# How the rows of two heads of W_o are split over the transfer engines, and x is loaded in four pieces

## The chip, the cores and the metric

The kernel runs on one core of a Trainium2 chip. The core has five compute queues that the profile names PE (TensorE, matrix multiplication), PEld (its weight loads), DVE (VectorE), ACT (ScalarE) and POOL (GpSimd), and SP, whose queue in this kernel does nothing but issue transfers. Transfers between the chip's memory (HBM) and the core's on-chip memory are carried by 16 transfer engines, which the profile calls the core's 16 DMA engines. Each works through its own share of the issued transfers.

The metric is device time in microseconds (us) of one execution. The time given for a kernel is the median over several executions.

## The reference, cut to what matters

One decoding step of a transformer block for two sequences (B = 2, one token each, D = 512): attention over a cache of 8192 positions with 32 heads of 128, and then a gated feed-forward layer of width 1376. Everything is bfloat16.

```python
def _A_ref(x, k_cache, v_cache, wq, wo):          # k_cache, v_cache: 2 x 32 x 8192 x 128
    q = (x @ wq).reshape(B, 1, 32, 128).transpose(0, 2, 1, 3)
    scores = einsum("bhqd,bhkd->bhqk", q, k_cache) * 128 ** -0.5
    o = einsum("bhqk,bhkd->bhqd", softmax(scores), v_cache)
    return o.transpose(0, 2, 1, 3).reshape(B, 1, 4096) @ wo
...
def _B_ref(x, W_gate, W_up, W_down):
    gate, up = x @ W_gate, x @ W_up
    return (gate * (gate > 0) * up) @ W_down
...
h  = x + _A_ref(layernorm(x), k_cache, v_cache, wq, wo)
h2 = h + _B_ref(layernorm(h), W_gate, W_up, W_down)
```

The caches are 2 x 128 MiB and each byte is read once. W_o is 4096 x 512: rows 128*h to 128*h + 127 belong to head h.

## The kernel before, in words

**Stages.** The caches come as 15 tiles of four heads each (8 MiB of K and 8 MiB of V a tile, 64 KB for each of the 128 partitions), and the last four heads of the second sequence as two half tiles, called p0 and p1 in the code. Three buffers of 64 KB per partition hold them in turn. For each tile DVE multiplies K by the query (`products`, L375), adds along the head dimension by halving (`scores`, L393 and L395), TensorE does a part of the positions itself (`scores_pe`), ACT takes exponentials, and TensorE multiplies with V (`values`, L446). When the caches are through, the weights W_o, W_gate, W_up and W_down are loaded into parts of the buffers that have come free, the attention's output is multiplied with W_o (`attend_set`, L502, and `attend`, L509), and the feed-forward layer follows: W_gate (`g_ps`, L686), W_up (`u_ps`, L686) and W_down (`d_ps`, L719).

**Order.** The order of every instruction on every queue is written out by hand in the source (`tc.manual_schedule()`). A transfer is issued when SP reaches it in its queue and the buffer that it writes is free; from there its packets stand in the transfer engines' own queues behind those issued earlier. There are eight semaphores for the completion of transfers, which the 56 transfers of the program use in turn; a transfer that finds its semaphore not yet at rest waits on SP for the earlier one.

**x.** x (2 x 512) is loaded as five rows onto two partitions, issued from ACT's queue (L190): per sequence pieces of 256 elements, the last piece of the second sequence cut into two of 128. TensorE transposes it (L238), the layer norm and the projection with W_q follow, and the first product with K waits for the projected query (`qrep`).

**W_o.** The rows are loaded in sets of heads (`SETS`: 16, 8, 4 and 2 heads, then heads 30 and 31 alone). In a set of n heads partition p holds n successive rows of W_o, so that each partition reads one contiguous piece of n KB; `load_set` (L567) issues it as 128 rows. The attention's output has to be laid out in the same way: `spread` (L481, one DVE instruction for each set and sequence) writes a head's column times a pattern of zeros and ones (`quot`), and `lay_rows` (L492, L496) multiplies that with the pattern `rest` on TensorE and copies the result to `orow`. Heads 30 and 31 are loaded plainly, row r of the head on partition r, and need no such layout. Head 31's load (L590) is written with its rows in four groups of 32, `[[P // 4 * D, 4], [D, P // 4], [1, D]]`; the groups follow each other without a gap in memory.

**W_down.** Its last chunk is loaded in three pieces of 32 partitions (L616), the other ten chunks in sets of 5, 3, 1 and 1 (L621).

Of the kernel before, what the change touches and what calls it, by code (L numbers as in the profile page):

```python
# [8 lines left out]
ALU = mybir.AluOpType  # L9
# [4 lines left out]
def _free(t, offset, dims):  # L14

    return bass.AP(tensor=t.tensor, offset=t.offset + offset, ap=[t.ap[0]] + [list(d) for d in dims])


def _dram(t, offset, dims):
    return bass.AP(tensor=t.tensor, offset=t.offset + offset, ap=[list(d) for d in dims])  # L20
# [3 lines left out]
def kernel(  # L24
# [13 lines left out]
    nc = tc.nc  # L38
    P = nc.NUM_PARTITIONS
    B, Sq, D = A_x.shape  # L40
    _, Hkv, Sk, Dh = A_k_cache.shape
    Hq = A_wq.shape[1] // Dh
# [24 lines left out]

    SETS = [(0, 16, 0), (16, 8, 16), (24, 4, 24), (28, 2, 28)]
    HM = 30
    SROWS = [n for _, n, _ in SETS]  # L70


# [15 lines left out]
    ocol = front.tile([P, Hq, B], bf16)  # L88
# [5 lines left out]
    qrep = consts.tile([P, LASTQ + 2, Dh], bf16)  # L94
# [17 lines left out]
    hm = consts.tile([P, FC, B], bf16)  # L112
    quot = {r: consts.tile([P, Dh // r], bf16, name=f"quot{r}") for r in SROWS}
    rest = {r: consts.tile([P, r], bf16, name=f"rest{r}") for r in SROWS}
    orow = [consts.tile([P, r, B], bf16, name=f"orow{k}") for k, r in enumerate(SROWS)]
    sel = consts.tile([B, B, P // 2], bf16)
# [8 lines left out]
    wo = bufs[0][:, HALF:TILE]  # L125
# [34 lines left out]
    def load_tile(cache, s, dst, pieces=1):  # L160
        h = NH * s.g + (0 if s.quad else 2 * s.k)
        n = s.nt * Dh
        w = n // pieces
        for k in range(pieces):
            nc.sync.dma_start(
                out=dst[:, k * w:(k + 1) * w], in_=_dram(cache, (s.b * Hkv + h) * Sk * Dh + k * w, [[n, P], [1, w]]),
            )

    def ln_cols(src, dst_bkc, pfx):

        m_ps = ps.tile([P, B, KC], f32, tag="mx")
        nc.tensor.matmul(out=m_ps, lhsT=mean_w, rhs=src, start=True, stop=True)
        mean = small.tile([P, B], f32, tag=pfx + "mean")
        nc.vector.tensor_reduce(out=mean, in_=m_ps, axis=AXIS.X, op=ALU.add)
        dev = small.tile([P, B, KC], f32, tag=pfx + "dev")
        nc.vector.tensor_tensor(out=dev, in0=src, in1=_free(mean, 0, [[1, B], [0, KC]]), op=ALU.subtract)
        sq = small.tile([P, B, KC], f32, tag=pfx + "sq")
        nc.vector.tensor_tensor(out=sq, in0=dev, in1=dev, op=ALU.mult)
        v_ps = ps.tile([P, B, KC], f32, tag="mx")
        nc.tensor.matmul(out=v_ps, lhsT=mean_w, rhs=sq, start=True, stop=True)  # L180
        rstd = small.tile([P, B], f32, tag=pfx + "rstd")
        nc.vector.tensor_reduce(out=rstd, in_=v_ps, axis=AXIS.X, op=ALU.add)
        nc.scalar.activation(out=rstd, in_=rstd, func=ACT.Sqrt, bias=eps_col, scale=1.0)
        nc.vector.reciprocal(out=rstd, in_=rstd)
        nc.vector.tensor_tensor(out=dst_bkc, in0=dev, in1=_free(rstd, 0, [[1, B], [0, KC]]), op=ALU.mult)

    with tc.manual_schedule():

        for b, k, n in ((0, 0, 2), (0, 2, 2), (1, 0, 2), (1, 2, 1), (1, 3, 1)):
            nc.scalar.dma_start(  # L190
                out=xr[b:b + 1, k * P:(k + n) * P], in_=_dram(A_x, b * D + k * P, [[D, 1], [1, n * P]]),
            )
# [9 lines left out]
            out=nscale, in_=nscale, compare_op=ALU.not_equal, fill=-SCALE,  # L202
# [5 lines left out]
            out=ident_f, in_=ident_f, compare_op=ALU.not_equal, fill=1.0,  # L208
# [4 lines left out]
            out=sel, in_=sel, compare_op=ALU.not_equal, fill=1.0,  # L213
# [9 lines left out]
            out=pick, in_=pick, compare_op=ALU.not_equal, fill=1.0,  # L223
# [17 lines left out]
        ln_cols(xc, xn.rearrange("p c b -> p b c"), "l1")  # L241
        for r in SROWS:
            nc.vector.tensor_reduce(out=rest[r], in_=_free(ident, 0, [[1, r], [r, P // r]]), axis=AXIS.X, op=ALU.max)
# [4 lines left out]
        for g0 in range(0, NQ, 4):  # L248
            for n0 in range(NH * g0 * Dh, NH * (g0 + 4) * Dh, 4 * Dh):
                q_ps = ps2.tile([B, 4 * Dh], f32, tag="o")  # L250
                for c in range(KC):
                    nc.tensor.matmul(  # L252
                        out=q_ps, lhsT=xn[:, c, :], rhs=wq_sb[:, c, n0:n0 + 4 * Dh], start=(c == 0), stop=(c == KC - 1),
                    )
                nc.vector.tensor_copy(qrow[:, n0:n0 + 4 * Dh], q_ps)
            for b in range(B):
                r_ps = ps2.tile([P, 4, Dh], f32, tag="tp")
                for j in range(NH):
                    nc.tensor.matmul(
                        out=r_ps[j * (P // NH):(j + 1) * (P // NH)], lhsT=sel[:, b, 0:P // NH],  # L260
# [5 lines left out]
        for j in range(2):  # L266
            nc.tensor.matmul(
                out=r_ps[j * (P // 2):(j + 1) * (P // 2)], lhsT=sel[:, B - 1, :],
# [116 lines left out]
        def scores(s):  # L385

            scol = scols[s.i]
            width = Dh
            while width > 8:
                half = width // 2  # L390
                lo = _free(s.kt, s.na * Dh, [[Dh, s.nv - s.na], [1, half]])
                hi = _free(s.kt, s.na * Dh + half, [[Dh, s.nv - s.na], [1, half]])
                nc.vector.tensor_tensor(out=lo, in0=lo, in1=hi, op=ALU.add)  # L393
                width = half
            nc.vector.tensor_reduce(  # L395
                out=scol[:, s.na:s.nv], in_=_free(s.kt, s.na * Dh, [[Dh, s.nv - s.na], [1, 8]]), axis=AXIS.X, op=ALU.add,
            )
            pms[s.i] = small.tile([P, 1], f32, tag="pm", name="pm", bufs=2)
            nc.vector.tensor_reduce(out=pms[s.i], in_=scol, axis=AXIS.X, op=ALU.max)  # L399
# [76 lines left out]
        def spread(k, b):  # L476

            h0, n, _ = SETS[k]
            nq = Dh // n
            sp = qrep[:, B * k + b, :]  # L480
            nc.vector.tensor_tensor(  # L481
                out=_free(sp, 0, [[nq, n], [1, nq]]), in0=_free(ocol, h0 * B + b, [[B, n], [0, nq]]),
                in1=_free(quot[n], 0, [[0, n], [1, nq]]), op=ALU.mult,
            )
            return sp

        def lay_rows(k, sps, scalar=False):

            r = SROWS[k]
            or_ps = ps.tile([P, B, r], f32, tag="mx")  # L490
            for b in range(B):
                nc.tensor.matmul(out=or_ps[:, b, :], lhsT=sps[b], rhs=rest[r], start=True, stop=True)  # L492
            if scalar:
                nc.scalar.activation(out=orow[k], in_=or_ps.rearrange("p b c -> p c b"), func=ACT.Copy)
            else:
                nc.vector.tensor_copy(orow[k], or_ps.rearrange("p b c -> p c b"))  # L496

        def attend_set(k, r0=0, r1=None):
            for c0 in range(r0, SROWS[k] if r1 is None else r1):
                for c in range(KC):  # L500
                    at = (SETS[k][2] + c0) * D + c
                    nc.tensor.matmul(  # L502
                        out=att_ps[:, c, :], lhsT=_free(wo, at, [[KC, P]]), rhs=orow[k][:, c0, :],
                        start=(k == 0 and c0 == 0 and c == 0), stop=False, skip_group_check=True,
                    )
# [9 lines left out]
        for i in range(Q):  # L515
# [21 lines left out]
            half = s.nt // VG // 2  # L537
# [27 lines left out]
        def load_set(k):  # L565
            h0, n, at = SETS[k]
            nc.sync.dma_start(  # L567
                out=wo[:, at * D:(at + n) * D], in_=_dram(A_wo, h0 * Dh * D, [[n * D, P], [1, n * D]]),
            )
# [14 lines left out]

        scores_pe(p0, values_and_sums)
        load_tile(A_v_cache, p1, p1.vt)
        for k in range(1, len(SETS)):
            load_set(k)
        nc.sync.dma_start(out=wo[:, HM * D:(HM + 1) * D], in_=_dram(A_wo, HM * Dh * D, [[D, P], [1, D]]))
        nc.sync.dma_start(  # L590
            out=wo[:, (HM + 1) * D:Hq * D], in_=_dram(A_wo, (HM + 1) * Dh * D, [[P // 4 * D, 4], [D, P // 4], [1, D]]),
        )
        scores(p0)

        def first():
# [15 lines left out]
        for w, src in ((0, B_W_gate), (1, B_W_up)):  # L611
            nc.sync.dma_start(
                out=wgu[:, w].rearrange("p c f -> p (c f)"), in_=_dram(src, 0, [[KC * F, P], [1, KC * F]]),
            )
        for q0 in range(AGAIN, P, AGAIN):
            nc.sync.dma_start(  # L616
                out=wd_sb[q0:q0 + AGAIN, FC - 1, :], in_=_dram(B_W_down, (F - P + q0) * D, [[D, AGAIN], [1, D]]),
            )
        for f0, n in FSETS[:-1]:
# [10 lines left out]
            out=z2_ps, lhsT=ones, rhs=_free(zc, ((B - 1) * NQ + groups[Q][1]) * NH, [[1, nb]]), start=True, stop=True,  # L630
# [6 lines left out]
        diagonals(Q)  # L637
        exponentials(p1)
        normalise(Q)
        sps = [[spread(k, b) for b in range(B)] for k in range(1, len(SETS))]  # L640
        nc.gpsimd.tensor_tensor(out=parts3, in0=ident[0:3 * B, 0:B], in1=ident[0:3 * B, B:2 * B], op=ALU.add)  # L641
        nc.gpsimd.tensor_tensor(out=parts3, in0=parts3, in1=ident[0:3 * B, 2 * B:3 * B], op=ALU.add)
        half = p1.nt // 2
# [8 lines left out]
        for k in range(1, len(SETS)):  # L652
            attend_set(k)
        for h in range(HM, Hq):
            attend(h)
# [38 lines left out]
        for c in range(KC):  # L694
            nc.tensor.transpose(hT_ps[:, c, :], hb[:, c].rearrange("p k b -> p (k b)"), ident)
        nc.scalar.activation(
            out=hrow.rearrange("q (p c) -> q p c", c=KC), in_=hT_ps.rearrange("q c p -> q p c"), func=ACT.Copy,
# [9 lines left out]
            out=gate, in0=g_ps, scalar=0.0, in1=_free(rvar, 0, [[0, FC], [1, B]]), op0=ALU.max, op1=ALU.mult,  # L707
# [59 lines left out]
```

## Time and profile before

| | us |
|---|---|
| Time, median of 3 executions (lowest, highest) | 659.27 (658.90, 659.71) |
| The profiled execution's own time | 659.39 |
| Its span, first to last instruction | 657.5 |
| DVE busy | 558.1 (85%) |
| PE busy | 352.1 (54%) |
| Idle time of DVE ahead of L375, put to K's transfer | 44.9 |
| Bytes moved | 281.37 MB, mean 428 GB/s |

How to read the profile: times are microseconds from the start of the span. In the chain of waits, each row gives a start, a duration and what it was: an instruction group by its line, or a transfer that something waited for ("DMA tile<-in_A_x_dram"), or an issue on a queue ("SPq", "ACTq"). A row of the timeline gives start, duration, engine, line, operation, and in square brackets how long the engine had been idle before it and for whom. The table of windows gives the busy time of each engine in a stretch, the granted TensorE clock, the share of the 16 transfer engines' time that was busy, and GB/s. The trace also records every packet of every transfer (start, duration, size) and, for each transfer, the times at which the transfer engines that carried it reported their shares as landed.

### The profile page before, as it was taken

What the parts mean: (1) busy time and instruction counts of PE and PEld (TensorE: products, weight loads), DVE (VectorE), ACT (ScalarE), POOL (GpSimd) and SP (SyncE); (2) the same over time, 40 slices, a digit from 0 to 9 for tenths busy, and PEclk for the clock granted to TensorE, in tenths of its full rate; (3) what the DMA queues carried; (4) which work ended last, traced back from release to release, by engine and by line L of the source; (5) the groups of instructions that cost most, each with busy time, mean ns of one, the idle gap of its engine ahead of it and who ended that gap; (6) DMA issues with size and microseconds to landing.
All of it is one profiled execution on the core that took longest, in us unless ns stands there. A gap on an engine that the chain in (4) does not pass through costs nothing.

```text
span 657.5 us, 5117 instructions
## 1 busy us (share of the span) xinstructions
PE 352.1 (54%) x2118; PEld 158.9 (24%) x2118; DVE 558.1 (85%) x252; ACT 123.6 (19%) x337; POOL 24.1 (4%) x36
## 2 busy tenths in 40 slices
PE   0730934809175380926539092552918458291997
PEld 0310311304022130312204031220403224030456
DVE  0599697988979799897979989796997969999982
ACT  0230030200203020030301103030210304201870
POOL 3080000000000000000000000000000000000020
PEclk9975775958778596877959687695968869686895
DMA  9999999999999999999999999999999999999997
GB/s 383 447 444 447 387 440 443 447 399 444 439 443 436 419 436 435 439 439 436 423 443 424 439 440 427 447 416 443 439 423 440 423 443 436 423 444 413 425 425 291
DMA packets 6948, 281.37 MB, mean 428 GB/s; under 512 B 809, under 2 KB 1422, under 8 KB 1934
## 3 DMA queue, kind: packets, MB, share of 16 engines
q1 hardware_dynamic: 6916, 281.06, 99.1%
q8 instruction: 16, 0.26, 0.1%
q14 instruction: 6, 0.05, 0.0%
q10 hardware_dynamic: 10, 0.00, 0.0%
HBM read 281.05 MB, written 0.00 MB: 427 GB/s over the span
## 4 chain that ended last, share of the span: by engine, by line
DVE 42%; DMA 37%; PE 18%; ACT 1%; issue 1%; ACTq 0%; SPq 0%; DVEq 0%
DMA tile<-in_A_k_cache_dram 30%; DVE tile L375 19%; DVE tile L393 18%; PE pv_ps L446 16%; DMA tile<-in_A_wo_dram 4%; DVE scol L395 2%; DMA tile<-in_A_x_dram 2%; DMA tile<-in_B_W_down_dram 1%; PE q_ps L252 1%; DVE pgq L420 1%; ACT ecol L415 1%; DVE pm L399 1%; DVE qrep L395 0%; DVE pm L410 0%; DVE hmax L412 0%
## 5 line engine op out<-in xcount | busy, mean ns | idle before, releaser
L446 PE MATMUL pv_ps<-tile,pgq 128*16 128x512 bf16 x960 | 244.3, 421 | 235.8 <-DVE pgq L420 223.2
L375 DVE TENSOR_TENSOR tile<-tile,qrep 128x29696 bf16<-128x29696 bf16 (+3 forms) x16 | 232.4, 14524 | 44.9 <-DMA tile<-in_A_k_cache_dram 44.9
L393 DVE TENSOR_TENSOR tile<-tile 128x14848 bf16<-128x14848 bf16 (+7 forms) x68 | 236.4, 3477 | 2.2
L446 PEld LDWEIGHTS <-pgq 128*16 128x16 bf16 x960 | 91.6, 97 | 378.1 <-DVE pgq L420 234.5
L451 ACT ACTIVATE pv<-pv_ps 16x512 f32<-16x512 f32 (+1 forms) x16 | 9.4, 589 | 243.7 <-PE pv_ps L446 243.6
L350 ACT ACTIVATE tile<-t_ps 128x1024 bf16<-128x1024 bf16 x53 | 52.6, 1022 | 12.6 <-PE t_ps L349 12.1
L415 ACT ACTIVATE ecol<-scol,nmax 128x256 bf16<-128x256 f32 x14 | 7.1, 508 | 196.1 <-DVE nmax L414 196.1
L340 PE MATMUL row_ps<-tile,qz 128*24 128x512 bf16 (+1 forms) x98 | 30.1, 389 | 18.0 <-ACT tile L350 17.9
L349 PE MATMUL t_ps<-ident,tile 128*128 128x128 bf16 x424 | 32.3, 229 | 13.0 <-DMA tile<-in_A_k_cache_dram 13.0
L349 PEld LDWEIGHTS <-tile 128*128 128x128 bf16 x424 | 25.8, 103 | 28.1 <-issue 14.2
L395 DVE TENSOR_REDUCE scol<-tile 128x232 f32<-128x1856 bf16 (+1 forms) x14 | 28.9, 2067 | 0.5
L641 POOL TENSOR_TENSOR tile<-ident 6x2 bf16<-6x2 bf16 x1 | 2.1, 2147 | 583.5 <-ACT tile L381 583.5
L420 DVE TENSOR_TENSOR pgq<-ecol,ownb 128x1024 bf16<-128x1024 bf16 x15 | 10.4, 692 | 10.3 <-ACT ecol L415 10.3
L381 ACT ACTIVATE tile<-tile 128x128 bf16<-128x128 bf16 x60 | 17.6, 293 | 1.9 <-DVE tile L375 1.9
L281 POOL COPY qzp<-qTs 128x4 bf16<-128x4 bf16 x1 | 15.0, 14982 | 26.1 <-DVE qTs L276 26.1
L375 DVE TENSOR_TENSOR tile<-tile,qpair 128x4096 bf16<-128x4096 bf16 (+3 forms) x4 | 15.5, 3883 | 0.0
L340 PEld LDWEIGHTS <-qz 128*24 128x24 bf16 (+1 forms) x98 | 7.9, 92 | 27.6 <-issue 22.7
L239 DVE CAST xc<-x_ps 128x8 f32<-128x8 bf16 x1 | 0.2, 167 | 15.5 <-PE x_ps L238 15.5
L367 ACT ACTIVATE scol<-sc_ps 32x24 f32<-32x24 f32 (+1 forms) x56 | 11.7, 209 | 7.7 <-PE sc_ps L362 7.2
L362 PE MATMUL sc_ps<-ident_f,tile 24*128 24x24 f32 (+2 forms) x68 | 7.2, 220 | 11.1 <-ACT tile L358 11.1
L358 ACT ACTIVATE tile<-row_ps 24x512 f32<-24x512 f32 (+2 forms) x17 | 10.0, 586 | 13.5 <-PE row_ps L340 13.5
L381 ACT ACTIVATION_READ_ACCUMULATOR tile<-tile 128x1 f32 x60 | 11.2, 186 | 0.0
(133 smaller groups left out, 143.8 us busy)
## 6 DMA issues: line engine op xcount, KB each, us to landing
tile<-in_A_k_cache_dram SPq DMA_DIRECT2D x2, 4096.0 KB
tile<-in_A_v_cache_dram SPq DMA_DIRECT2D x2, 4096.0 KB, 19.6
tile<-in_A_wq_dram SPq DMA_DIRECT2D x1, 4096.0 KB, 12.2
tile<-in_A_wo_dram SPq DMA_DIRECT2D x1, 2048.0 KB
tile<-in_B_W_gate_dram SPq DMA_DIRECT2D x1, 1376.0 KB, 22.8
tile<-in_B_W_up_dram SPq DMA_DIRECT2D x1, 1376.0 KB
tile<-in_A_wo_dram SPq DMA_DIRECT2D x1, 1024.0 KB, 23.8
tile<-in_B_W_down_dram SPq DMA_DIRECT2D x1, 640.0 KB
```

What stands on the lines that cost most here:

```text
L281: nc.gpsimd.tensor_copy(qzp[:, :, 6:8], qTs[:, B - 1, Hq - NH:Hq].rearrange("p (k j) -> p k j", j=2),)
L340: nc.tensor.matmul(out=row_ps, lhsT=z, rhs=s.kt[:, (nv + c0 + k) * Dh:(nv + c0 + k + 4) * Dh], start=(u == 0), stop=(u == U - 1),)
L349: nc.tensor.transpose(t_ps[:, k, :], s.kt[:, t * Dh:(t + 1) * Dh], ident)
L350: nc.scalar.activation(out=s.kt[:, (nv + c0) * Dh:(nv + c0 + TPC) * Dh], in_=t_ps.rearrange("p t s -> p (t s)"), func=ACT.Copy,)
L367: nc.scalar.activation(out=scols[s.i][r, nv:s.nt].rearrange("p (u t) -> p t u", t=4), in_=sc_ps[r, :, :, j], func=ACT.Copy,)
L375: nc.vector.tensor_tensor(out=kv, in0=kv, in1=_free(s.qr, 0, [[0, n], [1, Dh]]), op=ALU.mult)
L381: nc.scalar.activation(out=kv, in_=kv, func=ACT.Copy, accum_out=scols[s.i][:, t:t + 1])
L393: nc.vector.tensor_tensor(out=lo, in0=lo, in1=hi, op=ALU.add)
L395: nc.vector.tensor_reduce(out=scol[:, s.na:s.nv], in_=_free(s.kt, s.na * Dh, [[Dh, s.nv - s.na], [1, 8]]), axis=AXIS.X, op=ALU.add,)
L415: nc.scalar.activation(out=ecol, in_=scols[s.i], func=ACT.Exp, scale=SCALE, bias=nmax, accum_out=zs[:, s.b, s.g:s.g + 1],)
L420: nc.vector.tensor_tensor(out=s.pg, in0=_free(ecol, 0, [[VG, s.nt // VG], [0, NH], [1, VG]]), in1=_free(ownb, 0, [[0, s.nt // VG], [VG, NH ...
L446: nc.tensor.matmul(out=pv_ps[s.i][r, :], lhsT=s.pg[:, u].rearrange("p j t -> p (j t)"), rhs=s.vt[:, u * VG * Dh:(u + 1) * VG * Dh], start= ...
```

## The change

- x is loaded in four pieces of 256 elements; the two of 128 become one.
- The load of heads 28 and 29 (`SETS[3]`, 128 rows of 2 KB) is split into two transfers. Head 28's 64 rows of 2 KB go to partitions 0 to 63 as before. Head 29's 64 rows of 2 KB go to partitions 64 to 127 in another order: the source is read as 4 groups of 16 rows, where group g takes every fourth row, and group g lands on 16 successive partitions.
- Heads 30 and 31 are both loaded plainly as 128 rows of 1 KB.
- A new function `spread_last` writes the output's layout for heads 28 and 29 to match: one DVE instruction for head 28 and one for head 29, each for both sequences, in place of the two `spread` instructions of that set (one for each sequence).

```diff
+    LAST, BY = len(SETS) - 1, 4
...
-        for b, k, n in ((0, 0, 2), (0, 2, 2), (1, 0, 2), (1, 2, 1), (1, 3, 1)):
+        for b, k, n in ((0, 0, 2), (0, 2, 2), (1, 0, 2), (1, 2, 2)):
             nc.scalar.dma_start(
                 out=xr[b:b + 1, k * P:(k + n) * P], in_=_dram(A_x, b * D + k * P, [[D, 1], [1, n * P]]),
...
+        def spread_last():
+
+            h0, n, _ = SETS[LAST]
+            half, by = Dh // n, Dh // n // BY
+            both = qrep[:, B * LAST:B * LAST + B, :]
+            nc.vector.tensor_tensor(
+                out=_free(both, 0, [[Dh, B], [1, half]]), in0=_free(ocol, h0 * B, [[1, B], [0, half]]),
+                in1=_free(quot[n], 0, [[0, B], [1, half]]), op=ALU.mult,
+            )
+            nc.vector.tensor_tensor(
+                out=_free(both, half, [[Dh, B], [1, by], [by, BY]]), in0=_free(ocol, (h0 + 1) * B, [[1, B], [0, by], [0, BY]]),
+                in1=_free(quot[n], 0, [[0, B], [BY, by], [1, BY]]), op=ALU.mult,
+            )
+            return [both[:, b, :] for b in range(B)]
...
-        for k in range(1, len(SETS)):
+        for k in range(1, LAST):
             load_set(k)
-        nc.sync.dma_start(out=wo[:, HM * D:(HM + 1) * D], in_=_dram(A_wo, HM * Dh * D, [[D, P], [1, D]]))
+        h0, n, at_o = SETS[LAST]
+        half, row = P // n, n * D
         nc.sync.dma_start(
-            out=wo[:, (HM + 1) * D:Hq * D], in_=_dram(A_wo, (HM + 1) * Dh * D, [[P // 4 * D, 4], [D, P // 4], [1, D]]),
-        )
+            out=wo[0:half, at_o * D:at_o * D + row], in_=_dram(A_wo, h0 * Dh * D, [[row, half], [1, row]]),
+        )
+        nc.sync.dma_start(
+            out=wo[half:P, at_o * D:at_o * D + row],
+            in_=_dram(A_wo, (h0 + 1) * Dh * D, [[row, BY], [BY * row, half // BY], [1, row]]),
+        )
+        for h in range(HM, Hq):
+            nc.sync.dma_start(out=wo[:, h * D:(h + 1) * D], in_=_dram(A_wo, h * Dh * D, [[D, P], [1, D]]))
...
-        sps = [[spread(k, b) for b in range(B)] for k in range(1, len(SETS))]
+        sps = [[spread(k, b) for b in range(B)] for k in range(1, LAST)] + [spread_last()]
```

## The prediction, on record before the changed kernel ran

> **What bounds the kernel now.** I read the page's queues first, then the windows by stage, the chain of waits, the timeline around its last links, and then the trace's landings.
>
> ```profile
> q1 hardware_dynamic: 6916, 281.06, 99.1%
> q8 instruction: 16, 0.26, 0.1%
> q14 instruction: 6, 0.05, 0.0%
> ...
> 33.00:630.00 597.00, 316.81 (x1602) 135.44 (x1600) 535.96 (x189) 108.48 (x275) 14.54 (x1) 0.75 1.00 433
> 630.00:651.30 21.30, 18.17 (x348) 14.52 (x346) 11.50 (x33) 8.67 (x51) 3.66 (x2) 0.72 0.99 410
> 651.30:654.60 3.30, 3.15 (x88) 2.62 (x89) 0.83 (x5) 0.00 (x0) 0.00 (x0) 0.50 0.50 191
> 654.60:657.50 2.90, 0.28 (x4) 0.09 (x3) 0.56 (x2) 0.54 (x2) 0.00 (x0) 0.50 0.00 1
> ```
>
> The transfer engines are full (share 1.00) until 651.3. In the 3.3 us after that only half of them still work (0.50, 191 GB/s), and then none. DVE's 85% is no bound: its longest waits are for K. So the time is the time of the transfer engine that ends last, plus a tail. The end of the chain says the same:
>
> ```profile
> 643.73 0.35 SPq L621
> 644.08 0.05 issue
> 644.18 9.77 DMA tile<-in_B_W_down_dram
> 653.94 0.04 issue
> 653.99 0.60 PE d_ps L719 x15
> ...
> 654.61 0.33 PE d_ps L719 x4
> ```
>
> The last four products start at 654.61. The trace records 16 landings of each 128-row transfer, one for each engine. Of those I list five transfers:
>
> ```
> heads 28-29  640.61 .64 .66 .66 .78 641.15 | 642.11 .16 .41 .42 | 643.40 .54 .55 .61 .65 .66
> head 30      640.95 .98 641.00 .04 .18 .50 | 642.43 .47 .74 .75 | 643.71 .85 .86 .92 .96 .99
> head 31      641.32 .34 .37 .38 .52 .85    | 642.77 .81 643.06 .07 | 644.04 .19 .20 .25 .30 .32
> W_up         647.86 .90 .91 .91 648.04 .55 | 649.69 .89 .90 | 650.93 651.10 .15 .21 .22 .27 .29
> W_down, last 651.57 .62 .62 .62 .84 652.08 | 653.25 .33 .34 | 654.34 .45 .47 .48 .52 .55 .57
> ```
>
> Six engines end by 652.08, three by 653.34, seven by 654.57. They drift apart because the 16 blocks of q8 (PE's own instructions, 16 KB) fall on eight engines in turn: the first V tile lands at 51.10 to 51.52 on 15 engines and at 53.13 on the one that had carried a block at 36.8. So each block costs its engine about 1.5 us, and most of the eight carry two in time to matter. Head 31, written in four groups of 32 rows, landed 16 times: the groups join without a gap, and the load ran on 16 engines.
>
> **The change part by part.** Sums go against the profiled execution (659.39 us: span 657.5 and 1.9 around it), which lies 0.12 above the median 659.27 and inside the runs' 658.90 to 659.71.
>
> *Heads 28 and 29.* From the landing of heads 24-27 (first at 639.98) to that of heads 28-29 (640.61), an engine moves eight 2 KB rows in 0.63 us: 0.079 a row. Eight 1 KB rows take 0.34 to 0.37 (heads 30, 31). Head 28 on all engines is 4 rows, 0.32 us; heads 30 and 31 cost what they did. The new order of head 29 (every fourth row, four groups that don't join) is carried by four engines, 16 rows each: 1.26 us. So twelve engines end 0.63 - 0.32 = 0.31 us earlier, and four end 0.32 + 1.26 - 0.63 = 0.95 later. The bytes are the same; what matters is who carries them. If the four are among the nine early ones, the last of them ends at 653.34 + 0.95 = 654.29 or before, and the late seven at 654.57 - 0.31 = 654.26. The last landing moves by -0.28 to -0.31. No row shows a load on four engines. One engine would take 64 rows, 5.06 us (+4.75 for it); sixteen, as for head 31, nothing. I take four, the number of the source's groups, as head 31 with one joined group took 16 and the two-row output landed twice (656.68, 656.71).
>
> *Does PE follow?* The gain counts only if PE is free that much earlier.
>
> ```profile
> 650.44 0.60 PE L700 MATMUL v_ps<-sq,mean_w 128*128 128x8 f32 x2
> 651.33 1.58 PE L686 MATMUL u_ps<-hn,tile 128*128 128x2 bf16 x44 [0.30 <-DMA tile<-in_B_W_up_dram]
> 653.08 1.81 PE L719 MATMUL d_ps<-tile,hm 128*2 128x128 bf16 x44
> ```
>
> PE is idle for 0.30 us ahead of W_up, whose last landing goes from 651.29 to 650.98. So u_ps starts 0.29 earlier at most, at 651.04, and the products with W_down follow from 653.08 - 0.29 = 652.79. Forty of the 44 took 1.53 us with their waits (653.08 to 654.61), which gives 654.32 for the last four, against 654.30 to 654.33 by the landing. Both limits give -0.28 to -0.31; I take -0.3. Next to be late is PE's chain behind v_ps, which has no slack left.
>
> *x in four pieces.*
>
> ```profile
> 0.74 1.64 ACTq L190 DMA_DIRECT2D tile<-in_A_x_dram  x5
> 2.11 12.96 DMA tile<-in_A_x_dram
> 30.96 41.50 DMA tile<-in_A_k_cache_dram
> 32.41 15.08 DVE L375 TENSOR_TENSOR tile<-tile,qrep 128x28672 bf16<-128x28672 bf16 x1
> ```
>
> The five pieces landed at 1.96, 7.74, 10.19, 12.62 and 15.07: on their one engine each packet of x takes turns with a 32 KB packet of W_q (1.21 us), two turns a piece. Without the fifth, x is there at 12.62, 2.45 earlier. W_q's last landing is 12.96, and the layer norm takes from 15.20 to 18.56, so the projection starts at about 16.1 and the query is ready 2.45 earlier. DVE's first product then waits for K's first tile, which landed at 32.26: it starts 0.1 earlier. That is worth nothing, for K's next tiles come at the pace of full transfer engines (1.00 in the window). If that cover were gone it would be 2.45. The engine of x is spared two packets (0.03). ACT's queue is shorter by one issue, 0.33, ahead of a table load that nothing waits for until 17.82.
>
> *SP and the semaphores.* One issue more (0.43 to 0.47 at L589). SP reached W_gate's issue at 620.4 and waited 4.5 us there; an odd shape that cost it 4 us more would still be hidden, and behind that stand transfers that land until 644. The one x piece less makes up for the one W_o piece more in the turn of the eight semaphores, so from head 30 on each transfer has the one it had. But the second and third W_down pieces (L616) now wait for heads 24-27 and head 28 in place of heads 16-23 and heads 24-27. The third goes out at 643.35 (640.61 to 643.66, less 0.31) rather than 643.04, and L621 with it 0.3 later, at about 644.1. The earliest engine needs its first row when W_up and the small pieces are through, at 648.45: 4 us of cover.
>
> *spread_last.* Two DVE instructions for two, of 128 elements each as before (L481: 0.28 each). Strided writes may cost more; a strided reduce of 128 (L243) took 0.28 to 0.38, so 0 to 0.1 each. They end by 640.2, and PE comes to their product at 641.16: 0.9 of cover. Without it, 0.2.
>
> The sum: -0.3 on 659.27 gives 659.0.
>
> **The rivals.**
>
> *B, the four engines include a late one.* Then W_up and W_down end there 0.95 later: 659.27 + 0.95 = 660.2. It decides from the point where one of the four ends after 653.6 (654.57 - 0.95). For it: seven of sixteen do, and the profile doesn't number the engines. Against it: x was carried by one engine and the output by two, which suggests that a short transfer always falls on the same first few, and I followed the engine of x through the trace's packets, each of which starts where the one before it on its engine ends: it carried no block of q8, though where two engines run in step they can be mistaken for each other. [...]
>
> *C, fewer than four engines, or smaller packets.* One engine: from 651.57 + 4.75 = 656.32, 1.75 above 654.57 (the earliest engine), to +4.75 (a late one): 661.0 to 664.0. For it: this transfer's two sides have different shapes, which no row shows. Against it: both have 2 KB rows.
>
> *N, the change does nothing.* All on 16 engines, as with head 31 before: 659.3. Against it: the groups no longer join. [...]
>
> *X, the 2.45 us of x come through:* 656.8. For it: x's landing stands in the chain with 12.96 us. Against it: K's tile at 32.26 and the full transfer engines.
>
> **How the numbers follow.** The chances: the forecast 0.54 (659.0, its own range 658.6 to 659.4 by the scatter of the runs), B 0.22, C 0.11, X 0.08, N 0.05. This kernel's measurement can tell about 0.2% from no change, 1.3 us: 657.95 to 660.59. Faster is X, 0.08. Slower is C and a quarter of B (0.37 away from its value), 0.17. The rest, 0.75, is within. The range 658.6 to 661.0 holds the forecast, N, B and the lower end of C; X and the rest of C, about 0.16, are left out.
>
> **What would show it.** Head 29's load lands on four engines and heads 28, 30 and 31 on sixteen; W_down's last landings have seven at about 654.26 and four moved up by 0.95; u_ps waits for W_up no longer or by a hair; x lands at 12.6 and L375 starts at 32.3; L616 ends and L621 starts 0.3 later with nothing behind them. It is wrong if the last landing is later than 654.57 (B, C), if head 29 lands other than four times, or if DVE's first product starts well ahead of 32.2.

## The result, and the profile after

| | before | after |
|---|---|---|
| Time, median (lowest, highest), us | 659.38 (658.90, 659.71), 11 runs | 661.00 (660.65, 661.32), 11 runs |
| Ratio after/before, 95% interval | | 1.0024 (1.0015 to 1.0034) |
| The profiled execution's time and span, us | 659.39, 657.5 | 660.72, 658.9 |
| Last landing of W_down, us | 654.57 | 655.95 |

The changed kernel is 1.6 us slower, where 0.3 us faster was forecast. The last landing came 1.38 us later and the span grew by 1.4, so the loss is there before the last transfer is. The windows of the changed kernel, in the columns of the table in the prediction (the last three are the granted TensorE clock, the busy share of the transfer engines and GB/s):

```profile
33.00:630.00 597.00, 315.89 (x1603) 135.80 (x1602) 536.33 (x191) 108.63 (x276) 0.00 (x0) 0.75 1.00 433
630.00:651.30 21.30, 17.54 (x347) 14.09 (x345) 11.38 (x29) 8.03 (x50) 3.52 (x2) 0.71 0.99 377
651.30:654.60 3.30, 2.25 (x58) 2.03 (x62) 1.02 (x6) 0.41 (x1) 0.00 (x0) 0.50 0.80 294
654.60:658.90 4.30, 1.55 (x44) 0.93 (x36) 0.56 (x2) 0.54 (x2) 0.00 (x0) 0.50 0.11 38
```

Until 630 us the transfers run as before (433 GB/s in both). From there to 651.3 the transfer engines are as busy as before (0.99), but move 377 GB/s where it was 410. So a share of 0.99 does not say that the bytes flow. What was not moved by then fills the next windows: 294 GB/s to 654.6, before 191.

The end of the chain of waits, and the timeline of PE ahead of it (L639, L709 and L742 of the changed kernel are L616, L686 and L719 of the one before):

```profile
645.15 0.31 SPq L639
645.46 0.05 issue
...
646.03 9.29 DMA tile<-in_B_W_down_dram
655.32 0.04 issue
655.36 0.62 PE d_ps L742 x13
...
655.99 0.33 PE d_ps L742 x4
```

```profile
649.00 1.58 PE L709 MATMUL g_ps<-hn,tile 128*128 128x2 bf16 x44 [1.55 <-DMA tile<-in_B_W_gate_dram]
...
652.65 1.58 PE L709 MATMUL u_ps<-hn,tile 128*128 128x2 bf16 x44 [1.03 <-DMA tile<-in_B_W_up_dram]
...
654.45 1.82 PE L742 MATMUL d_ps<-tile,hm 128*2 128x128 bf16 x44
```

The chain ends in the same links as before, 1.38 us later: the last four products start at 655.99 (before 654.61), 0.04 us behind the landing. PE is now idle 1.55 us for W_gate and 1.03 us for W_up, where it had waited 0.30 for W_up. So PE has slack, and the transfers alone set the end. The landings of five transfers of the changed kernel:

```
head 28      640.31 .34 .44 .52 .59 .79 | 642.52 .71 .74 .81 | 643.91 644.55 .70 .72 645.10 .14
head 29      642.10 642.84 | 644.97 645.31
head 31      first 641.01, last 645.68          (before 641.32 to 644.32)
W_up         first 649.00, last 652.61          (before 647.86 to 651.29)
W_down, last 652.65 653.02 .07 .19 .95 | 654.34 | 655.36 .61 .62 .77 .77 .78 .78 .81 .92 655.95
```

Head 29 did land on four engines, two early ones and two of the middle ones. But the early engines, too, are late now: the first W_up landing comes at 649.00, 1.14 us after that of before, although twelve engines carry fewer bytes than before. The trace's packets show where it goes. Mean length of one packet from 630 us on, in ns, with its bytes:

```
                      8 KB   4 KB   2 KB   11,008 B (W_gate, W_up)
before                 313    159     84    420
after                  331    206    121    464
```

The 2 KB packets are those of heads 28 and 29: all 84 ns before, up to 285 after. But those of 4 KB (heads 24 to 27), which the change does not touch, went from 159 to 206 as well. To weigh this I add up, over all packets and engines, the time above the usual length of their size (16, 8, 5, 4, 3, 2, 1 KB: 611, 309, 196, 159, 121, 84, 46 ns; 11,008 B: 413). From 632 to 647 us this excess is 0.5 us before and 28.8 after, 1.8 us for each of the 16 engines. That is about the size of the loss, though it is a mean over the engines, while the last engine decides. Only 4.7 of the 28.8 us lie in the packets of heads 28 and 29 themselves; 2.8 lie in heads 16 to 23, 6.1 in heads 24 to 27, 4.5 in heads 30 and 31, and 10.7 in W_gate and W_up.

### The profile page after: what moved, and what is told of

It is laid out like the page before. It is cut to its first block, busy times and chain, and to the rows that moved or that the text cites. A ratio compares the mean times of both kernels' runs of the same rounds, so it can differ in the third digit from the quotient of the medians.

```text
span 658.9 us, 5117 instructions
## 1 busy us (share of the span) xinstructions
PE 351.5 (53%) x2118; PEld 159.2 (24%) x2118; DVE 558.6 (85%) x252; ACT 123.5 (19%) x337; POOL 9.1 (1%) x36
## 4 chain that ended last, share of the span: by engine, by line
DVE 42%; DMA 37%; PE 18%; ACT 1%; issue 1%; SPq 0%; ACTq 0%; DVEq 0%
DMA tile<-in_A_k_cache_dram 30%; DVE tile L376 19%; DVE tile L394 18%; PE pv_ps L447 16%; DMA tile<-in_A_wo_dram 4%; DVE scol L396 2%; DMA tile<-in_A_x_dram 2%; PE q_ps L253 1%; DMA tile<-in_B_W_down_dram 1%; DVE pgq L421 1%; ACT ecol L416 1%; DVE pm L400 1%; DVE qrep L396 0%; DVE pm L411 0%; DVE hmax L413 0%
## 5 line engine op out<-in xcount | busy, mean ns | idle before, releaser
L253 PE MATMUL q_ps<-tile,xn 128*2 128x512 bf16 x32 | 9.7, 468 | 1.0 <-DVE xn L186 1.0
## 6 DMA issues: line engine op xcount, KB each, us to landing
tile<-in_A_wo_dram SPq DMA_DIRECT2D x1, 2048.0 KB, 24.1
```

What stands on the lines that cost most here:

```text
L253: nc.tensor.matmul(out=q_ps, lhsT=xn[:, c, :], rhs=wq_sb[:, c, n0:n0 + 4 * Dh], start=(c == 0), stop=(c == KC - 1),)
```

## The experiments

My theory after the result: what costs is that heads 28 and 29 are now written by loads that each reach only half of the partitions, 0 to 63 and 64 to 127. The expectations call this the port theory, or the theory of the ports; no run shows a port, and the name stands for no more than that the packets of such loads, and of the loads around them, take longer. The rivals are the four engines, the way the rows are read from DRAM, the split into more loads, and x. All ratios are against the kernel before, run beside the experiment.

### The parts of the change one by one

x alone, in four loads:

```diff
-        for b, k, n in ((0, 0, 2), (0, 2, 2), (1, 0, 2), (1, 2, 1), (1, 3, 1)):
+        for b, k, n in ((0, 0, 2), (0, 2, 2), (1, 0, 2), (1, 2, 2)):
```

> The kernel before with x in four loads and nothing else. Every theory of the W_o loads says 659.4 us (ratio 0.999 to 1.001): x lands near 12.7 in place of 15.07, DVE's first product with K starts near 32.3, and the landings at the end stay at 651.6 to 654.6. A theory that the earlier x, or the shifted turn of the semaphores, costs the 1.6 us says 660.5 or more.

Measured: 659.41, ratio 1.0001 (0.9991 to 1.0010); packets of 2 KB at 84 ns. x is worth nothing that these runs can tell.

The changed kernel with head 29 in plain order, so that sixteen engines carry it, and `spread` as before; the halves stay:

```diff
-            in_=_dram(A_wo, (h0 + 1) * Dh * D, [[row, BY], [BY * row, half // BY], [1, row]]),
+            in_=_dram(A_wo, (h0 + 1) * Dh * D, [[row, half], [1, row]]),
```

> The changed kernel with head 29's rows in plain order, so that both halves (64 partitions each) are carried by sixteen engines; the layout of the output is made by the old function. Port theory (packets that go to only half of the partitions get in each other's way, and in the way of other loads under way): the 2 KB packets take over 0.100 us on average in place of 0.084, packets stretch by 8 us or more in sum over the engines, and the time is 659.7 to 660.6. Four-engine theory (only the four engines with 16 rows each cost time): 0.084, no stretch, 659.1 to 659.5. Stride theory (every fourth row of 2 KB is slow to read): no stretch, 659.1 to 659.5.

Measured: 660.78, ratio 1.0022 (1.0013 to 1.0032), 0.2 above the range forecast for the halves. Without any load on four engines nearly the whole slowdown is still there. 2 KB packets 102 ns, 4 KB 190, excess 21.7 us, last landing 656.32. The four engines add 7 us of excess (28.8 against 21.7), but 661.00 against 660.78 is too little to tell apart.

The kernel before with heads 28 and 29 in one load of 128 rows, read from rows that lie 8 KB apart (other rows of W_o, so these two heads' weights are wrong):

```diff
+            out=wo[:, 28 * D:30 * D], in_=_dram(A_wo, 0, [[8 * D, P], [1, 2 * D]]),
```

> The kernel before, but heads 28 and 29 are loaded from rows that lie 8 KB apart (128 rows of 2 KB, on all 128 partitions, sixteen engines); the weights of these two heads are therefore the wrong rows. Stride theory: the 2 KB packets take 0.100 us or more on average. Port theory and four-engine theory: 0.084 as before, and the time stays at 659.4 within 0.4.

Measured: 659.21 in a single execution (before 659.33), all 2 KB packets at 84 ns. Reading with a stride costs nothing here that the packets show.

The dealing without the halves: head 28 on all partitions, and head 29's 128 KB as 16 rows of 8 KB on partitions 0 to 15, carried by four engines behind W_up (not used in the products, which read head 28's columns twice):

```diff
+        nc.sync.dma_start(
+            out=bufs[2][0:16, HALF + 2 * KC * F:HALF + 2 * KC * F + 8 * D],
+            in_=_dram(A_wo, 29 * Dh * D, [[8 * D, 4], [32 * D, 4], [1, 8 * D]]),
+        )
```

> The kernel before, but the load of heads 28 and 29 is replaced by 128 rows of 1 KB on all partitions (sixteen engines) and, behind W_up's load, 16 rows of 8 KB on partitions 0 to 15 in four groups of four (four engines, 1.24 us each); head 29's weights are thereby left out of the result and head 28's loaded in another order. The bytes are the same. Port theory: hardly any packet stretches before 645, the sixteen move 0.29 earlier and the four 0.95 later; if a late engine is among the four, 660.1 to 660.5, which leaves 0.5 to 0.9 of the change's 1.6 us to the stretched packets. Four-engine theory: the whole 1.6 us is here too, 661.0. If none of the four is a late engine: 659.1.

Measured: 659.20, ratio 0.9997 (0.9987 to 1.0007). Head 29 landed four times, at 648.98, 649.00, 650.81 and 650.93: again two early and two middle engines. Packets were stretched no more than in the kernel before (usual lengths 309 ns for 8 KB and 159 for 4 KB; excess 0.6 us, before 0.5, which in both is nearly all one 8 KB packet of 855 ns). So four engines that do not end last can carry head 29 without a loss. The gain of 0.3 us that the forecast gave is not shown: W_down's last landing was 654.37 (before 654.57), but the kernel with x alone, whose loads of W_o are those of before, had it at 654.90 in its profile, so 0.2 us lies within the scatter.

### The halves alone, and twice

The kernel before with its one load of heads 28 and 29 cut in two, each row where it was:

```diff
+        for q0 in (0, P // 2):
+            nc.sync.dma_start(
+                out=wo[q0:q0 + P // 2, at_o * D:at_o * D + row], in_=_dram(A_wo, h0 * Dh * D + q0 * row, [[row, P // 2], [1, row]]),
+            )
```

> The kernel before, with the one load of heads 28 and 29 (128 partitions x 2 KB) put as two loads of 64 rows x 2 KB, the first to partitions 0 to 63, the second to 64 to 127; every partition gets the row that it had. [...] Rival (what costs is how the dealt rows are read from DRAM, or that heads 30 and 31 come one by one): 659.3, packets at 84 and 159 ns.

Measured: 661.00, ratio 1.0025 (1.0015 to 1.0036), +1.63; 2 KB packets 100 ns, 4 KB 188. I had estimated +1.0 to +1.5, most of the 1.45 (660.78 - 659.33) of the run with the halves on sixteen engines. This one edit, with x, the order of the rows, the sixteen engines and heads 30 and 31 as before, makes the whole loss. Its excess is 19.0 us, 1.2 for each engine, where the changed kernel with the same time and the same last landing (655.95) has 28.8. So the excess tells where packets are stretched, and the time only roughly. The same cut in the load of heads 24 to 27 instead (4 KB rows, 512 KB), with heads 28 and 29 in their one load:

```diff
-        for k in range(1, len(SETS)):
-            load_set(k)
+        load_set(1)
+        h0, n, at_o = SETS[2]
...
+        for q0 in (0, P // 2):
+            nc.sync.dma_start(
+                out=wo[q0:q0 + P // 2, at_o * D:at_o * D + row], in_=_dram(A_wo, h0 * Dh * D + q0 * row, [[row, P // 2], [1, row]]),
+            )
+        load_set(3)
```

> The kernel before, with the load of heads 24 to 27 (128 partitions x 4 KB) put as two loads of 64 rows x 4 KB to partitions 0 to 63 and 64 to 127, and heads 28 and 29 in their one load. Twice the bytes go by halves that did in the changed kernel. Theory of the ports: twice the delay, +2.5 to +3.5 us against before, about 660.3 to 662.8, stretched packets of 4 KB above 250 ns. Rival (a fixed cost for each half load, whatever its size): +1.0 to +1.6 us, 660.4 to 661.0.

Measured: 662.41, ratio 1.0050 (1.0034 to 1.0065); 4 KB packets 245 ns, 2 KB (heads 28 and 29, in one load to all partitions) 128, excess 42.4 us. 256 KB by halves cost 1.63 us (661.00 - 659.37), 512 KB 3.04: with two half loads in both, the delay grows with the bytes. The stretch of 630 to 647 us in the kernel before, in the changed kernel, with 256 KB and with 512 KB by halves:

```profile
630.00:647.00 17.00, 14.84 (x296) 11.58 (x294) 10.00 (x23) 8.09 (x50) 3.66 (x2) 0.78 0.99 418
```

```profile
630.00:647.00 17.00, 14.79 (x296) 11.66 (x294) 10.21 (x21) 7.86 (x49) 3.52 (x2) 0.76 0.99 371
```

```profile
630.00:647.00 17.00, 14.91 (x293) 11.90 (x291) 9.77 (x21) 7.55 (x47) 4.00 (x2) 0.73 1.01 394
```

```profile
630.00:647.00 17.00, 14.19 (x290) 11.39 (x289) 9.54 (x20) 7.31 (x45) 4.00 (x2) 0.73 1.00 352
```

The share stays at 0.99 to 1.01, and the rate falls from 418 to 371, 394 and 352 GB/s.

### Which partitions

Is it loads of 64 rows, or these partitions? Two programs differ in nothing but the partitions to which two loads of 64 rows x 2 KB go, 32 to 95 in one and 0 to 63 in the other. I expected no stretch on 32 to 95, which no run had shown so far. The first:

```diff
+        row, mid = n * D, slice(P // 4, 3 * P // 4)
+        for q0, to in ((0, wo[mid, at_o * D:at_o * D + row]), (P // 2, bufs[2][mid, TILE - row:TILE])):
+            nc.sync.dma_start(out=to, in_=_dram(A_wo, h0 * Dh * D + q0 * row, [[row, P // 2], [1, row]]))
```

and the same with both loads on partitions 0 to 63. The second load goes to the third big tile because there is no room for a tile of its own (the pool that would hold it needs 15.53 KB per partition then, and 15.47 are left). In a third program, head 28 goes to all partitions and only head 29 to 64 rows:

```diff
+        nc.sync.dma_start(out=wo[:, at_o * D:at_o * D + D], in_=_dram(A_wo, h0 * Dh * D, [[D, P], [1, D]]))
+        nc.sync.dma_start(
+            out=bufs[2][P // 2:P, TILE - row:TILE], in_=_dram(A_wo, (h0 + 1) * Dh * D, [[row, P // 2], [1, row]]),
+        )
```

> The kernel before, with the load of heads 28 and 29 put as two loads of 64 rows x 2 KB that both go to partitions 32 to 95 (the first to W_o's own columns, the second to the last columns of the third big tile, and the products with heads 28 and 29 read the columns of heads 26 and 27 instead, so their weights are left out). Shape, rows, bytes of a row, engines and source are those of the run with the two halves; only the partitions differ. [...] Rival (a load of 64 rows is slow as such, or two loads in place of one): as slow as the run with the halves, 660.8 to 661.2, with the same stretched packets.

> The same program as the run on partitions 32 to 95, word for word, but both loads go to partitions 0 to 63. [...] Rival (what differs from the halves is only the place in the third tile or the products left out): as fast as the run on partitions 32 to 95.

> The kernel before, with head 28 in a load of its own to all partitions (128 rows x 1 KB) and head 29 in a load of 64 rows x 2 KB to partitions 64 to 127 by sixteen engines (into the third tile; the products read the columns of heads 26 and 27, so these weights are left out). Half of the bytes that the changed kernel sends by halves. Measured so far: 256 KB by halves +1.6 us, 512 KB +3.0. Theory of the ports, delay in proportion to the bytes: +0.6 to +0.9, 659.9 to 660.3. Rival (only the meeting of two half loads, one for each half, costs): 659.3.

Measured: 677.07, 679.84 and 679.14; ratios 1.0273 (1.0258 to 1.0289), 1.0314 (1.0298 to 1.0329) and 1.0298 (1.0281 to 1.0315). All three are 17.7 us and more above before (659.35), far beyond anything expected, for a reason that I had overlooked: the last columns of the third tile still held V, which the load overwrote (8 of 256 blocks, in 64 partitions), so PE's product with V waited for it, as the timeline of the run on 32 to 95 shows:

```profile
643.18 1.01 PE L446 MATMUL pv_ps<-tile,pgq 128*16 128x512 bf16 x2 [17.68 <-DMA tile<-in_A_wo_dram]
```

The times can't be set against before, then. But the transfers ran, and the first two programs are the same but for the partitions. On 32 to 95 every packet from 632 to 647 us had its usual length (2 KB 84 ns, 4 KB 159, excess 0.0 us) and W_down landed last at 654.13. On 0 to 63: 2 KB 117 ns, 4 KB 211, excess 32.8 us, last landing 656.90. With one half load of 128 KB: excess 11.3, last landing 655.43. So 0, 128 and 256 KB by halves gave landings at 654.13, +1.30 and +2.77.

To have a time that can be set against before, the pair once more with the two loads moved behind heads 30 and 31, where V is no longer read (the edit is that of the pair, one place further on, ahead of W_gate's load):

> The two loads of 64 rows x 2 KB to partitions 32 to 95 once more, but placed behind heads 30 and 31 and just ahead of W_gate, where the third tile's V is no longer read, so that nothing but W_gate stands behind them (weights of heads 28 and 29 left out of the products as there). The run with these loads further ahead had every packet at its usual length and the last landing of W_down at 654.13. Theory of the ports: the same here, 659.2 within 0.4, that is no change against before although 256 KB go by loads of 64 rows. Rival (loads of 64 rows cost time that the landings did not show): 660.5 to 661.

> The same program as the run on partitions 32 to 95 ahead of W_gate, word for word, with both loads on partitions 0 to 63. Theory of the ports: slower by the 2.8 us that parted the two earlier runs of this pair, 661.5 to 662.5, with the packets of the loads around it stretched. Rival (the 2.8 us came from what was read too late in that pair, not from the loads): 659.2.

Measured: partitions 32 to 95 659.65, ratio 1.0006 (0.9996 to 1.0015); 0 to 63 661.75, ratio 1.0035 (1.0021 to 1.0049). The two windows, 32 to 95 first:

```profile
630.00:647.00 17.00, 14.70 (x295) 11.47 (x293) 9.70 (x21) 7.91 (x49) 3.51 (x2) 0.78 0.99 414
```

```profile
630.00:647.00 17.00, 14.21 (x294) 11.26 (x291) 9.60 (x21) 7.41 (x45) 3.79 (x2) 0.76 0.99 369
```

414 against 369 GB/s, excess 0.5 against 28.5 us, last landing 654.60 against 656.27. The first is 0.42 us above before, a little more than the 0.4 that I had allowed, but its interval holds no change, and its last landing is that of before (654.57). Two loads of 64 rows cost nothing measurable on partitions 32 to 95 (the interval alone would leave room for 1.0 us, but no more packets are stretched than before), and 2.5 us (661.75 - 659.23) on 0 to 63.

The runs agree. With loads of 64 rows on 0 to 63 alone (excess 32.8 and 28.5 us), with one on 64 to 127 (11.3) and with one on each (19.0) the packets are stretched; with both on 32 to 95 they are not (0.0 and 0.5). They show that the partitions decide, not what the packets wait for.

### The one other place where packets are stretched

The kernel before has 3.1 us of excess from 647 to 657, around the three loads of 32 partitions for W_down's last chunk. In one load, with the 32 doubled rows nulled in `gate`:

```diff
-        for q0 in range(AGAIN, P, AGAIN):
-            nc.sync.dma_start(
-                out=wd_sb[q0:q0 + AGAIN, FC - 1, :], in_=_dram(B_W_down, (F - P + q0) * D, [[D, AGAIN], [1, D]]),
-            )
+        nc.sync.dma_start(out=wd_sb[:, FC - 1, :], in_=_dram(B_W_down, (F - P) * D, [[D, P], [1, D]]))
...
-        nc.vector.memset(wd_sb[0:AGAIN, FC - 1, :], 0.0)
+        nc.vector.memset(gate[0:AGAIN, FC - 1, :], 0.0)
```

> The kernel before, with the last chunk of W_down read by one load to all 128 partitions instead of three to 32 each, and the 32 doubled rows nulled in gate (a memset behind the gate's product) rather than in W_down. The three small loads are the one other place where the packets of the kernel before are stretched: about 3 us summed over the engines at 648 to 652 us, 0.2 for each, and their own rows take 0.61 us for each engine against 0.34 for one load. Theory of the ports: the last landing 0.3 to 0.5 us earlier than in the kernel before and the time 658.9 to 659.1. Rival (32 neighbouring partitions in turn over the whole cost nothing, or PE's products after the landing are the bound): 659.3.

Measured: 659.26, ratio 0.9999 (0.9990 to 1.0008), no change where 658.9 to 659.1 was forecast. The excess from 647 to 657 us went to 0.5. The profiled execution has its last landing at 654.01, and PE ends its products at 654.32:

```profile
650.66 1.58 PE L682 MATMUL u_ps<-hn,tile 128*128 128x2 bf16 x44 [0.25 <-DMA tile<-in_B_W_up_dram]
...
652.50 1.82 PE L716 MATMUL d_ps<-tile,hm 128*2 128x128 bf16 x44
```

That is 0.56 us earlier at the last landing, but this execution (658.88) was the fastest of its eleven. The medians differ by 0.11 us only (659.26 and 659.37). The stretch there is gone; that the time is shorter is not shown. Whether the 32 partitions or the three loads had stretched the packets was not tested apart. No version was shown to beat the kernel before.

## Why the prediction was wrong, and where it was right

**What bounds the kernel: right.** The last landing moved by 1.38 us and the span by 1.4.

**Who carries head 29: right.** Four engines, two early and two middle ones. The run with the dealing alone again had two early and two middle ones and lost nothing, so rival B, a late engine among the four, is out. That head 29 lies on four engines does not explain the loss: with sixteen it is nearly as large (660.78).

**The price of a packet: this step failed.** "Head 28 on all engines is 4 rows, 0.32 us; heads 30 and 31 cost what they did." The price of 0.079 us for a 2 KB row came from a load to all 128 partitions and was carried over to loads to 64 neighbouring ones. There a packet took 121 ns in the mean rather than 84, the 1 KB packets of heads 30 and 31 64 rather than 46 (16.3 us in 256 packets, before 11.8), and the loads around them, which the sum did not hold at all, lost more than heads 28 and 29 did: heads 24 to 27 took 206 rather than 159, W_gate and W_up 464 rather than 420. "The bytes are the same; what matters is who carries them" left out where they go. The term that should have stood there is the excess, 28.8 - 0.5 us over 16 engines, +1.77 for each, in place of none. With the forecast's -0.3 that makes +1.5; the last landing showed +1.38 and the medians +1.62. So close a sum is partly luck, for the halves alone lost as much with an excess of 19.0.

**The rivals.** C named the right side and, for another reason, the right size (its lower end is 661.0): its causes, a single engine or smaller packets, did not come about, as head 29 landed four times in rows of 2 KB. That the measured 661.00 lies at the upper end of the range, which was to take in that lower end of C, is luck. N, no change, would not have held with head 29 on sixteen engines either (660.78): as two loads to the halves, the same bytes to the same places are 1.63 us slower than as one load. The three W_down pieces, to 32 partitions each, landed 16 times each in the kernel before (648.05 to 651.90), like a load to all partitions, and yet stand in a stretch with 3.1 us of excess: 0.04 of it in the 1 KB packets, and the rest in W_up (1.7) and in the W_down loads behind the pieces (1.4). I had looked at how often they landed, not at how long the packets were.

**PE follows: right, and beside the point.** PE had more slack, not less (1.55 and 1.03 us of waits).

**x: right.** From the chain of waits and the timeline of DVE of the changed kernel:

```profile
1.82 10.92 DMA tile<-in_A_x_dram
...
29.41 42.77 DMA tile<-in_A_k_cache_dram
```

```profile
30.66 0.19 DVE L277 COPY qTs<-qT_ps 128x32 bf16<-128x32 bf16 x1 [0.26 <-PE qT_ps L276]
32.40 15.09 DVE L376 TENSOR_TENSOR tile<-tile,qrep 128x28672 bf16<-128x28672 bf16 x1 [1.55 <-DMA tile<-in_A_k_cache_dram]
```

x is there at 12.74 (forecast 12.62), the query 1.55 us before K's tile, and the first product starts at 32.40 instead of 32.41. That "the query is ready 2.45 earlier" was too much: its last copy starts at 30.66, before at 32.31, only 1.65 earlier. The projection on PE began 2.33 us earlier (16.23, before 18.56), but the query needed 0.68 us longer from there; why stays open. K's tile covers it all, and x alone is worth nothing (1.0001).

**SP, semaphores, spread_last: hidden, with sizes off.**

```profile
639.56 0.72 DVE L497 TENSOR_TENSOR qrep<-ocol,quot 128x128 bf16<-128x128 bf16 x1
```

```profile
619.80 4.98 SPq L615 DMA_DIRECT2D tile<-in_A_wo_dram  x2
629.35 0.33 SPq L635 DMA_DIRECT2D tile<-in_B_W_gate_dram  x1
639.00 0.33 SPq L635 DMA_DIRECT2D tile<-in_B_W_up_dram  x1
642.29 3.17 SPq L639 DMA_DIRECT2D tile<-in_B_W_down_dram  x3
```

The strided instruction of `spread_last` took 0.72 us, not 0.28 to 0.38; it ends at 640.28, and PE comes to its product at 640.80. W_gate was issued at 629.35 instead of 624.84 and W_up at 639.00 instead of 629.68. The prediction saw that with one W_o load more the W_down pieces wait for a later transfer, and overlooked that W_gate and W_up do so too. That stayed hidden: W_gate's packets start at 640.30, and its first landing is at 645.75. The third W_down piece went out at 645.15, not 643.35, since the transfers that it waits for were late; the first engine is through W_up at 649.00, so 3.9 us of cover were left.

## What to carry to other kernels

Where the transfer engines are full, ask of each load which partitions it writes, not only how many bytes, rows and engines it has: two loads to the two halves cost 1.6 us for 256 KB and 3.0 us for 512 KB against one load to all partitions, and 64 rows on partitions 32 to 95 cost nothing measurable. A price taken from a load to all partitions (84 ns for a packet of 2 KB) held for loads to 32 to 95 (84), and did not for loads to 0 to 63 (117) or to 0 to 63 and 64 to 127 (100 to 121). Read GB/s beside the busy share, for a share of 0.99 went with 418 and with 371 GB/s in the same 17 us, and read the lengths of the packets, which tell a slow place from a busy one (84 against 121 ns for 2 KB in those two runs).

## What the runs showed of the hardware that I had not expected

- The loads to partitions 0 to 63 and 64 to 127 stretched the packets of other loads too: heads 24 to 27 from 159 to 206 ns a packet, W_gate and W_up from 420 to 464. The engines stand 3 us and more apart (head 31 landed from 641.32 to 644.32 before the change), so some are in the half loads while others are still in the load before them or already in the next; that this is how the others' packets come to be stretched is my reading, not shown.
- The same shows on a small scale around three loads of 32 partitions: 3.1 us of excess around 96 KB of W_down, 0.5 when the chunk came in one load.
- Four engines were no burden by themselves: 128 KB on four of them in rows of 8 KB stretched the other packets no more than before (excess 0.6 us, before 0.5), at 659.20 us in place of 659.33.
- POOL's copy of the query into `qzp` took 14.98 us before and 0.19 after; POOL was busy for 24.1 and 9.1 us in all. x in four loads alone does the same (9.2). Before, the copy (32.56 to 47.54) stood beside DVE's first product (32.41 to 47.49); with the query earlier it is done at 31.1. The time did not change with it.
